# Three more matmuls in twelve attention steps of a fused kernel, one or two fewer in twenty-four

## The chip, the cores and the metric

The kernel runs on one core of a Trainium2 chip. The metric is the device time of one launch in microseconds (us), from the first instruction to the last. Engines are named as in the profile: PE is TensorE (matmuls), PEld its weight loads, DVE is VectorE, ACT is ScalarE, POOL is GpSimd, SP is SyncE, which issues most DMAs.

## The reference

A sparse attention over 8 batches and 8 heads is followed by a two-layer network. In the attention only scores within tau of their row's maximum survive. What is computed, without the set-up:

```python
scores = q @ k.T / sqrt(64)                      # q, k, v: (8, 8, 576, 64)
thresh = max(scores, -1) - tau                   # tau = 0.02
scores = where(scores >= thresh, scores, -1e9)
attn = exp(scores - max(scores, -1)); attn = attn / (sum(attn, -1) + 1e-9)
x = (attn @ v) reordered to (4608, 512)
h = x @ w_in                                     # (512, 2048)
g = h * tanh(softplus(h))
out = g @ w_out                                  # (2048, 512)
```

## The kernel before

**Tiles and steps.** The attention is cut into 288 tiles of 128 rows of q against all 576 keys: 8 batches, 4 pairs of heads in each, 9 tiles a pair. One loop with the number g (line 553) walks over them as a software pipeline. Every engine gets its work in program order: the class InOrder (line 83) chains each engine's instructions, so what stands behind a waiting instruction waits too.

**What PE gets in step g.** First the scores of tile g+1 (`begin`, into an s tile; pss has two of them). Then, in four steps of nine, the product of attention and v for an earlier tile (`product`, nine matmuls into a y tile, lines 406 to 415). Then a number of matmuls of the first product x @ w_in of the previous batch (`advance(stream, n)`, line 645). Last, from step 38 on, the four or five transposes of tile g-2 (line 649; pst has one buffer for them, tp, and one for t5).

**The first product as a stream.** `gemm1` (line 446) is a generator that yields after every matmul. An output tile h has 12 matmuls: four blocks of the inner dimension times three products, since x and w_in are each split in a high and a low part (xh, xl, w1h, w1l). A batch has 32 h tiles, 384 matmuls. After its twelfth matmul an h is copied to hst by ACT (`leave`, line 473). The table MIX_FIRST, MIX or MIX_LAST says how many matmuls step g takes; MIX_FIRST is for the first batch, whose stream runs in steps 42 to 77, and is read at g modulo 36:

```python
advance(stream, DRAIN if g >= NT else MIX_FIRST[(step + 6) % 36] if b == 1 else ...)
```

**What the other engines do in step g.** DVE takes the row maximum of tile g (st), the small operations on it, lo of tile g-3 (the low part of the transposed tile, which needs ACT's hi of the same tile), and p of tile g (the masked exponentials, which frees that tile's s). ACT makes hi and tk of tile g-3, the exponentials e of tile g, the copies x and yo of this step's y (`gather`, line 422), casts of loaded q, k and v, and at the end the copies hst of h tiles that ended in this step. POOL normalises p and makes low parts. Up to step 54 DVE, ACT and POOL also decode w_in into w1h and w1l (the tiles named dec).

**The buffers in question.** The pool psh has two PSUM buffers with the tag "ph". Every h and every y takes one of them, and it is free again once ACT has copied its content out (hst for an h, x and yo for a y).

```python
psh = outer.enter_context(tc.tile_pool(name="psh", bufs=2, space=PSUM))
y = psh.tile([P, 512], F32, name="y", tag="ph")
banks[c, f] = pool.tile([P, 512], F32, name="h", tag=tag)
```

**Behind the loop** w_out is decoded, the gate is applied and the second product (line 848) fills the rest of the span.

Of the kernel before, what the change touches and what calls it, by code (L numbers as in the profile page):

```python
# [64 lines left out]
    8: [(3, 128, 0, 128)],  # L65
}
MIX = (11, 12, 6, 9, 8, 13, 12, 14, 16, 6, 16, 4, 12, 4, 15, 5, 16, 13)
MIX_FIRST = (11, 12, 6, 9, 8, 13, 6, 14, 22, 6, 16, 4, 12, 4, 15, 9, 16, 13, 7, 12, 5, 10, 8, 13, 12, 14, 16, 6, 16, 4, 12, 4, 15, 5, 16, 13)
MIX_LAST = (12, 14, 16, 6, 16, 4, 12, 4, 15, 5, 16, 13, 11, 12, 6, 9, 8, 13, 12, 14, 16, 6, 16, 4, 12, 4, 15, 5, 16, 13, 11, 12, 6, 9, 8, 13)
DRAIN = 18  # L70
LAST = {1: 0, 4: 1, 6: 2, 8: 3}
# [87 lines left out]
def attention_moe(tc, q, k, v, tau, w_in, w_out, out):  # L159
# [3 lines left out]
    with ExitStack() as outer:  # L163
# [12 lines left out]
        with ExitStack() as first:  # L176
# [6 lines left out]
            with ExitStack() as att:  # L183
# [311 lines left out]
                def advance(stream, n):  # L495
                    for _ in range(n):
                        next(stream, None)
# [55 lines left out]
                for g in range(NT + 5):  # L553
# [88 lines left out]
                    if b >= 1:  # L642
                        if step == 0:
                            stream = gemm1(b - 1, batches.pop(b - 1))
                        advance(stream, DRAIN if g >= NT else MIX_FIRST[(step + 6) % 36] if b == 1 else MIX[g % 18] if b < B - 1 else MIX_LAST[step])
                    if g < len(WARM[1]):
# [252 lines left out]
```

## Time and profile before

| what | value |
|---|---|
| median of 3 runs | 1373.96 us |
| lowest and highest run | 1373.25, 1374.07 us |
| profiled execution, its own time | 1371.94 us |
| its span, first to last instruction | 1370.2 us |
| PE, DVE, ACT, POOL busy | 1352.5, 1000.6, 944.0, 774.0 us |
| steps 42 to 77 in the span | 137.5 to 257.3 us |

The profile is one execution on the chip. A row of its timeline gives the start in us from the span's start, the duration, the engine, the line of the kernel (L93 stands for every instruction recorded by the helper InOrder), the operation, output and inputs by the program's names without buffer numbers, the shape, how many equal instructions were merged (x4), and in brackets how long the engine sat idle before and what ended that. A row of the windows gives, for each engine, the busy time and in brackets the number of instructions, then PEclk, the granted TensorE clock as a share of 2.4 GHz, and the share of the DMA engines. The steps are found by DVE's row maxima (TENSOR_REDUCE), one in each step: step 42's starts at 137.48 us, step 78's at 257.32 us.

### The profile page before, as it was taken

How to read it: one execution, taken by the hardware profiler on the slowest of the kernel's cores; microseconds unless marked ns; L12 is line 12 of the kernel's file. 1: busy time of each engine (PE TensorE's matmuls, PEld its weight loads, DVE VectorE, ACT ScalarE, POOL GpSimd, SP SyncE). 2: the span in 40 equal slices, each digit the busy share in tenths (PEclk: the TensorE clock that was granted, in tenths of full speed). 3: DMA queues.
4: the chain of work that ended last, by engine and by line, in shares of the span. 5: the costliest groups of instructions: out<-in, count | busy, mean ns of one | idle time of the engine just before them, and what ended most of it. 6: DMA issues, size and time to landing. Idle time of an engine off the chain costs nothing. (4 is left out here: it accounts for less than half of the span.)

```text
span 1370.2 us, 27693 instructions
## 1 busy us (share of the span) xinstructions
PE 1352.5 (99%) x8839; PEld 1225.8 (89%) x8839; DVE 1000.6 (73%) x2976; ACT 944.0 (69%) x2106; POOL 774.0 (56%) x1115
## 2 busy tenths in 40 slices
PE   9998999999999999999999999999999999999999
PEld 7555899999999999999999999999987888888888
DVE  5999999999999999999999999957874332232210
ACT  5788788888888888888888888856555543443210
POOL 4778888778788787887887878732460000000000
PEclk9999999999999999999999999999999999999999
DMA  4333423333333233332332423128655553543310
GB/s 142 100 96 109 121 79 116 108 96 103 101 99 115 89 121 93 111 105 99 103 111 88 121 93 107 64 86 279 194 164 154 150 151 103 143 132 99 95 52 23
DMA packets 126017, 154.64 MB, mean 113 GB/s; under 512 B 23472, under 2 KB 109488, under 8 KB 125872
## 3 DMA queue, kind: packets, MB, share of 16 engines
q1 hardware_dynamic: 124720, 148.16, 36.2%
q10 hardware_dynamic: 1152, 4.72, 0.9%
q8 instruction: 70, 1.15, 0.3%
q14 instruction: 75, 0.61, 0.1%
HBM read 105.64 MB, written 47.19 MB: 112 GB/s over the span
## 5 line engine op out<-in xcount | busy, mean ns | idle before, releaser
L848 PE MATMUL o<-g,w2h 128*128 128x512 f32 (+1 forms) x1280 | 363.7, 370 | 0.6 <-DVE g L681 0.6
L93 PE MATMUL h<-xh,w1h 128*128 128x288 f32 x1024 | 302.3, 295 | 1.0 <-ACT hst L93 0.6
L93 PE MATMUL h<-xl,w1h 128*128 128x288 f32 x1024 | 302.2, 295 | 0.0
L93 PE MATMUL h<-xh,w1l 128*128 128x288 f32 x1024 | 302.2, 295 | 0.0
L93 POOL TENSOR_SCALAR p<-p,st 128x576 f32<-128x576 f32 x288 | 244.9, 850 | 58.6 <-DVE st L93 37.2
L848 PEld LDWEIGHTS o<-g,w2h 128*128 128x128 f32 x1280 | 231.6, 188 | 43.4 <-DVE g L681 1.1
L93 PE MATMUL s<-k,q 128*128 128x288 f32 (+1 forms) x1280 | 255.0, 324 | 7.9 <-DVE p L93 5.8
L93 DVE SCALAR_TENSOR_TENSOR p<-s,st,e 128x576 f32<-128x576 f32 x288 | 235.0, 816 | 20.6 <-ACT e L93 11.0
L93 ACT ACTIVATE e<-s,st 128x576 f32<-128x576 f32 x288 | 214.4, 744 | 35.5 <-DVE st L93 30.2
L848 PE MATMUL o<-g,w2l 128*128 128x512 f32 (+1 forms) x640 | 236.1, 369 | 0.0
L93 DVE TENSOR_REDUCE st<-s 128x1 f32<-128x576 f32 x288 | 216.6, 752 | 6.7 <-PE s L93 6.6
L93 PEld LDWEIGHTS s<-k,q 128*128 128x128 f32 (+1 forms) x1280 | 182.5, 189 | 37.4 <-DVE p L93 21.8
L93 DVE TENSOR_TENSOR lo<-tp,hi 128x512 fp32r<-128x512 f32 (+1 forms) x280 | 174.7, 632 | 48.0 <-ACT hi L93 41.0
L93 PEld LDWEIGHTS h<-xh,w1h 128*128 128x128 f32 x1024 | 192.6, 188 | 1.9 <-ACT hst L93 1.0
L93 PEld LDWEIGHTS h<-xh,w1l 128*128 128x128 f32 x1024 | 192.5, 188 | 0.0
L93 PEld LDWEIGHTS h<-xl,w1h 128*128 128x128 f32 x1024 | 192.5, 188 | 0.0
L93 PE MATMUL tp<-ident,p 128*128 128x128 f32 x1152 | 174.4, 274 | 3.5 <-DVE lo L93 2.3
L93 ACT CAST hi<-tp 128x512 fp32r<-128x512 f32 (+1 forms) x280 | 149.8, 546 | 36.4 <-PE tp L93 33.5
L681 DVE TENSOR_TENSOR g<-ht,g 128x1024 fp32r<-128x1024 f32 (+1 forms) x60 | 68.6, 1153 | 137.6 <-ACT g L680 137.6
L93 PEld LDWEIGHTS tp<-ident,p 128*128 128x128 f32 x1152 | 139.0, 140 | 13.6 <-issue 5.8
L676 ACT ACTIVATE ht<-ht 128x1024 f32<-128x1024 f32 (+1 forms) x60 | 60.2, 1003 | 115.9 <-DMA ht<-hd 114.5
L848 PEld LDWEIGHTS o<-g,w2l 128*128 128x128 f32 x640 | 120.3, 188 | 21.2
(87 smaller groups left out, 2226.7 us busy)
## 6 DMA issues: line engine op xcount, KB each, us to landing
hd<-hst SPq DMA_DIRECT2D x56, 576.0 KB, 3.3
r<-q SPq DMA_DIRECT2D x120, 160.0 KB, 2.3
r<-k SPq DMA_DIRECT2D x120, 160.0 KB, 2.3
ht<-hd SPq DMA_DIRECT2D x52, 288.0 KB, 3.3
r<-v SPq DMA_DIRECT2D x56, 160.0 KB, 2.3
dec<-w_in SPq DMA_DIRECT2D x32, 256.0 KB, 2.7
out_t<-ost SPq DMA_DIRECT2D x32, 256.0 KB, 2.9
g<-w_out SPq DMA_DIRECT2D x48, 128.0 KB, 2.8
```

The costliest lines, as they stand in the source:

```text
L93: made = method(*args, **kwargs)
L676: nc.scalar.activation(ht, ht, AF.Mish)
L681: engine.tensor_tensor(gl, ht, fv(gh), ALU.subtract)
L848: nc.tensor.matmul(o[:, :m], a, b, start=n == 0, stop=n == 3 * NF - 1)
```

## The change

Only the table MIX_FIRST changes. By the step that reads an entry: steps 42 to 47 and 72 to 77 (the table's entries 6 to 11 and 0 to 5) take three more matmuls each, steps 48 to 71 one or two fewer. The sum of the table goes from 384 to 385, while the stream has 384 matmuls, so step 77 takes 15 where its entry says 16. After step 47 the stream is 18 matmuls ahead of before, after step 59 one ahead, after step 71 seventeen behind. What each matmul computes does not change, and no wait, buffer or DMA is added.

```diff
-MIX_FIRST = (11, 12, 6, 9, 8, 13, 6, 14, 22, 6, 16, 4, 12, 4, 15, 9, 16, 13, 7, 12, 5, 10, 8, 13, 12, 14, 16, 6, 16, 4, 12, 4, 15, 5, 16, 13)
+MIX_FIRST = (14, 15, 9, 12, 11, 16, 9, 17, 25, 9, 19, 7, 10, 3, 13, 8, 14, 12, 5, 11, 4, 9, 6, 12, 10, 13, 14, 5, 14, 3, 10, 3, 13, 4, 14, 12)
```

PE's order at the end of step 43 before: the last matmuls of the step in an h tile (h_1987 is the second of the batch), the transposes (tp, t5), then the scores s of the next step. In brackets stands the engine whose semaphore an instruction waits for (Activation is ACT).

```order
L93 MATMUL h_1987<-xl_1479,w1h_96 128x288
L93 MATMUL tp_1996<-ident_79,p_1830 128x128 [waits DVE_49,PE_49,Pool_49]
L93 MATMUL tp_1996<-ident_79,p_1830 128x128 x3
L93 MATMUL t5_2001<-ident_79,p_1830 128x128
L93 MATMUL s_2003<-k10_1569,q0_1568 128x288 [waits DVE_49]
L93 MATMUL s_2003<-k20_1570,q0_1568 128x288
L93 MATMUL s_2003<-k10_1569,q0_1568 128x288
L93 MATMUL s_2003<-k20_1570,q0_1568 128x288
```

The same place after: the second h tile is complete, and a third one (h_2001) starts before the transposes.

```order
L93 MATMUL h_1987<-xh_1817,w1l_97 128x288
L93 MATMUL h_2001<-xh_752,w1h_96 128x288 [waits Activation_49]
L93 MATMUL h_2001<-xl_753,w1h_96 128x288
L93 MATMUL tp_2004<-ident_79,p_1830 128x128 [waits DVE_49,PE_49,Pool_49]
L93 MATMUL tp_2004<-ident_79,p_1830 128x128 x3
L93 MATMUL t5_2009<-ident_79,p_1830 128x128
L93 MATMUL s_2011<-k10_1569,q0_1568 128x288 [waits DVE_49]
L93 MATMUL s_2011<-k20_1570,q0_1568 128x288
L93 MATMUL s_2011<-k10_1569,q0_1568 128x288
```

What moved: six more h matmuls stand ahead of these transposes (three of step 42, three of step 43), and the first matmul of h_2001, which waits for ACT, stands ahead of the transposes and scores.

PE's order in step 67 before: the last matmul of a y tile (y_3318), four h matmuls, all of one h tile that ends there, then the transposes and the next scores.

```order
L93 MATMUL y_3318<-tk_3156,vs_2286 128x256
L93 MATMUL h_3299<-xh_1480,w1l_97 128x288
L93 MATMUL h_3299<-xh_1819,w1h_96 128x288
L93 MATMUL h_3299<-xl_1820,w1h_96 128x288
L93 MATMUL h_3299<-xh_1819,w1l_97 128x288
L93 MATMUL tp_3354<-ident_79,p_3182 128x128 [waits DVE_49,Pool_49]
L93 MATMUL tp_3354<-ident_79,p_3182 128x128 x3
L93 MATMUL t5_3359<-ident_79,p_3182 128x128
```

The same place after: three h matmuls, of which two end an h tile and the third starts the next.

```order
L93 MATMUL y_3306<-tk_3149,vs_2308 128x256 [waits Activation_49]
L93 MATMUL h_3285<-xl_1820,w1h_96 128x288
L93 MATMUL h_3285<-xh_1819,w1l_97 128x288
L93 MATMUL h_3340<-xh_754,w1h_96 128x288 [waits PE_49,Activation_49]
L93 MATMUL tp_3342<-ident_79,p_3175 128x128 [waits DVE_49,Pool_49]
L93 MATMUL tp_3342<-ident_79,p_3175 128x128 x3
L93 MATMUL t5_3347<-ident_79,p_3175 128x128
L93 MATMUL s_3349<-k11_2539,q1_2538 128x288 [waits DVE_49]
```

What moved: the boundary between two h tiles, which stood in the next step, now stands two matmuls behind y. The same form, an h that ends and one that starts behind a y of the same step, comes up in steps 47, 58, 67, 72 and 76 after, and in no step of 42 to 77 before.

## Rows read from the trace of the kernel before

**Rows 1.** The page, busy time of PE: us, share of the span, instructions.

```profile
PE 1352.5 (99%) x8839; PEld 1225.8 (89%) x8839; DVE 1000.6 (73%) x2976; ACT 944.0 (69%) x2106; POOL 774.0 (56%) x1115
```

**Rows 2.** Windows over steps 42–53, 54–59, 60–71, 72–77 (columns: see above).

```profile
137.50:184.40 46.90, 41.88 (x291) 39.27 (x291) 45.71 (x151) 37.81 (x99) 41.74 (x51) 0.95 0.36 109
184.40:201.90 17.50, 17.50 (x133) 17.11 (x133) 16.69 (x57) 15.00 (x36) 13.79 (x21) 1.00 0.25 73
201.90:239.10 37.20, 37.19 (x286) 36.51 (x285) 33.94 (x115) 31.88 (x79) 32.60 (x50) 1.00 0.39 118
239.10:257.30 18.20, 18.20 (x143) 18.20 (x141) 17.00 (x55) 15.45 (x36) 12.44 (x20) 1.00 0.22 75
```

**Rows 3.** Waits of PE, steps 42 to 59: us in total, times, longest.

```profile
PE s L93 <- DVE p L93: 3.8, 6, 1.2
PE tp L93 <- DVE lo L93: 1.1, 1, 1.1
```

**Rows 4.** Timeline of PE in step 43: start, duration (us), what, idle before.

```profile
143.03 0.30 PE L93 MATMUL h<-xh,w1h 128*128 128x288 f32 x1
...
144.75 0.29 PE L93 MATMUL h<-xl,w1h 128*128 128x288 f32 x1
146.12 0.63 PE L93 MATMUL tp<-ident,p 128*128 128x128 f32 x4 [1.08 <-DVE lo L93]
...
147.25 0.80 PE L93 MATMUL s<-k,q 128*128 128x288 f32 x4 [0.39 <-DVE p L93]
```

**Rows 5.** Timeline of ACT, end of step 43 and start of step 44.

```profile
145.22 0.74 ACT L93 ACTIVATE e<-s,st 128x576 f32<-128x576 f32 x1 [1.87 <-DVE st L93]
...
146.88 0.40 ACT L93 COPY hst<-h 128x288 f32<-128x288 f32 x1
147.17 0.59 ACT L93 CAST hi<-tp 128x512 fp32r<-128x512 f32 x1
```

**Rows 6.** Timeline of DVE, lo in steps 44, 50 and 64.

```profile
148.16 0.67 DVE L93 TENSOR_TENSOR lo<-tp,hi 128x512 fp32r<-128x512 f32 x1
...
171.27 0.69 DVE L93 TENSOR_TENSOR lo<-tp,hi 128x512 fp32r<-128x512 f32 x1 [0.43 <-ACT hi L93]
...
216.32 0.69 DVE L93 TENSOR_TENSOR lo<-tp,hi 128x512 fp32r<-128x512 f32 x1 [0.80 <-ACT hi L93]
```

**Rows 7.** Timeline of PE, transposes and scores behind steps 60 and 64.

```profile
205.58 0.60 PE L93 MATMUL tp<-ident,p 128*128 128x128 f32 x4
205.94 0.78 PE L93 MATMUL s<-k,q 128*128 128x288 f32 x4
...
217.94 0.60 PE L93 MATMUL tp<-ident,p 128*128 128x128 f32 x4
218.55 0.80 PE L93 MATMUL s<-k,q 128*128 128x288 f32 x4
```

**Rows 8.** PE and ACT, y's last matmul and yo, steps 67, 72, 76.

```profile
226.37 0.28 PE L93 MATMUL y<-tk,vs 128*128 128x256 f32 x1
227.08 0.36 ACT L93 COPY yo<-y 64x256 f32<-64x256 f32 x1
...
241.31 0.31 PE L93 MATMUL y<-tk,vs 128*128 128x320 f32 x1
242.09 0.42 ACT L93 COPY yo<-y 64x320 f32<-64x320 f32 x1
...
253.40 0.28 PE L93 MATMUL y<-tk,vs 128*128 128x256 f32 x1
254.20 0.36 ACT L93 COPY yo<-y 64x256 f32<-64x256 f32 x1
```

**Rows 9.** Timeline of PE, step 44, the h behind a wait for hst.

```profile
150.01 0.40 PE L93 MATMUL h<-xh,w1h 128*128 128x288 f32 x1
```

**Rows 10.** Windows around step 43 with the granted clock (PEclk), columns as above.

```profile
131.80:135.20 3.40, 1.42 (x8) 0.98 (x8) 3.31 (x11) 3.34 (x9) 2.19 (x4) 1.00 0.32 95
135.20:142.00 6.80, 5.68 (x24) 5.31 (x25) 6.71 (x23) 5.71 (x16) 6.80 (x10) 0.50 0.41 114
```


## The prediction

> **What bounds the kernel now.** I read the page's busy times first: TensorE (PE) is busy for 99% of the span [rows 1]. Busy PE is not the whole answer, so I next took the windows over steps 42 to 77, the only steps whose numbers change, cut at four places [rows 2]. They show two regimes. In 137.5 to 184.4 us (steps 42 to 53) VectorE (DVE) is busy 45.71 of 46.90 us and PE only 41.88: here w_in is still being decoded, and DVE sets the pace. From 184.4 us on PE has no idle time to speak of (17.50 of 17.50, 37.19 of 37.20, 18.20 of 18.20), yet DVE is close behind (33.94 of 37.20 in steps 60 to 71). Third, the waits of PE by cause: in steps 42 to 59 it sat idle 3.8 us for p of DVE (the score banks) and 1.1 us for lo of DVE (the transpose bank) [rows 3]. That idle time is what extra matmuls could fill.
>
> The pitch of one h matmul is the unit of everything: in step 43 fourteen of them start between 143.03 and 144.75 us, 13 pitches in 1.72 us, so 0.132 us each [rows 4].
>
> **The change in numbers.** By step number modulo 36, steps 42 to 47 get 18 more matmuls (2.38 us of PE), steps 48 to 59 get 17 fewer, steps 60 to 71 get 18 fewer, and steps 72 to 77 get 17 more (step 77 asks for 16, but only 15 of the 384 are left). Nothing is added to any engine, only moved, so the time changes by the waits of PE that appear less those that go. I went through the steps one by one, keeping three clocks (PE, ScalarE = ACT, DVE), with the durations of the trace.
>
> **Early, steps 42 to 59.** Step 42's three extra matmuls move step 43 by 0.40 us. In step 43 the third h tile now starts after 15 matmuls, at 143.03 + 0.40 + 15 x 0.132 = 145.41 us. psh has two buffers, both held by h tiles, and the one it needs was finished 12 matmuls earlier; ACT's copy of it is the last thing ACT does in the step, 146.88 to 147.28 us [rows 5], behind an exponential that waits for DVE and not for PE. So PE waits about 1.9 us there, in place of the wait for lo before the transposes (146.12 us) and the one for p before the scores (147.25 us) [rows 4]. Behind the waiting matmul are queued one more h, the transposes and the scores: the transposes start near 147.7 instead of 146.12 us, the scores near 148.2 instead of 147.25. The six matmuls found no gap. ACT's hi then starts near 148.35 instead of 147.17 us [rows 5], and DVE's lo near 148.95 instead of 148.16 us [rows 6]: DVE, the bound here, is 0.8 us late. Steps 44 to 47 add 12 x 0.132 = 1.58 us, which PE mostly cannot hide in steps 44 to 46 (it hardly waits there now), and in step 47 an h starts five matmuls after a y, of which more below. By step 48 I have PE's scores 1.4 us late and DVE 0.8 to 1.1 us. Steps 48 to 54 stay DVE-bound, and fewer matmuls there mostly lengthen PE's waits. DVE regains something where it now waits for hi (0.43 us at 171.27 [rows 6]), since transposes come earlier. In steps 54 to 59 PE has up to seven matmuls less to do than before, but DVE is busy 16.69 of 17.50 us [rows 2], so at most 0.8 us comes back, and step 58 has a new wait of 0.5. I carry **+0.45 us** into step 60. Bounds: -0.9 if the lead of seven matmuls at step 54 is kept whole and DVE loses nothing; +1.5 if DVE keeps its delay and the new waits come on top.
>
> **Middle, steps 60 to 71.** Eighteen matmuls fewer are 2.38 us of 37.20. Not all can be had: PE already waits for DVE before some scores (218.55 us, 0.61 us behind the transposes, where 0.36 is the pitch without a wait, as 205.94 less 205.58 shows [rows 7]; three more like it follow), and DVE's 33.94 us plus its own wait for hi (0.80 us at 216.32 [rows 6]) leave about 2 us. I take **-1.4 us**, bounds -0.9 and -2.4.
>
> **Late, steps 72 to 77.** PE has no slack here [rows 2], so 17 x 0.132 = **+2.25 us**.
>
> **The new wait: an h behind a y in the same step.** A y takes one of psh's two buffers while the other holds the open h. If that h ends and another starts in the same step, the new one needs the buffer of y or of the h just ended; ACT empties y first (x, then yo), and h after that. Before, no step does this; now steps 47, 58, 67, 72 and 76 do, 5, 5, 2, 4 and 2 matmuls behind y. Price from rows, as the end of yo less the start of y's last matmul, against PE's arrival. Step 67: 227.08 + 0.36 - 226.37 = 1.07 us, PE arrives after 0.12 + 2 x 0.132 = 0.38, wait 0.69 [rows 8]. Step 72: 242.09 + 0.42 - 241.31 = 1.20, arrival 0.15 + 4 x 0.132 = 0.68, wait 0.52 [rows 8]. Step 76: 254.20 + 0.36 - 253.40 = 1.16, arrival 0.38, wait 0.78 [rows 8]. With about 0.1 us each to start again (an estimate: the first h behind the one short wait for hst takes 0.40 us instead of 0.29 [rows 4, 9]) that is 0.8 + 0.6 + 0.9 = **+2.3 us**, all where PE is the bound; those of steps 47 and 58 are already in the early term. Behind each waiting h stand the transposes and scores of the step, so DVE and ACT fall back with PE. Bounds: 1.4 (step 67's falls into a stretch where DVE is late anyway, and step 72's half hidden) and 2.6.
>
> **The clock, a rule against the rows.** The granted clock fell to 0.50 (1.2 GHz) for 135.2 to 142.0 us [rows 10], behind a stretch in which PE made eight matmuls between its waits (busy 1.42 of 3.40 us); through the waits of steps 43 to 54, the longest 1.2 us [rows 3], it stayed at 1.00 (2.4 GHz): the mean of 0.95 in the first window [rows 2] is what those microseconds at 0.50 up to 142.0 make. The change makes one wait of 1.9 us there. The Trainium skill, page "TensorE: Matmul & The Clock Gate", section "A second HAM failure mode: psum-queue depth-cycling", says that a kernel cycling through PSUM buffers can idle PE briefly so often that its clock swings between the two levels; nothing in this trace shows waits on buffers doing that. By the rows I add nothing; as a rival it has a price below.
>
> **Sum.** 0.45 - 1.4 + 2.25 + 2.3 = +3.6 us. Later batches keep their numbers and PE has no slack to give it back. Against the profiled execution (span 1370.2, 1371.94 us in all) that is 1375.5 us; the median of the runs is 1373.96, 2.0 us above the profiled one, and the forecast is set on it: 1373.96 + 3.6 = **1377.6 us**, 0.26% slower.
>
> **Rivals.** (1) The lead pays: the 18 early matmuls fill PE's 4.9 us of idle time [rows 3], the lead of seven at step 54 is kept (-0.9), the middle gives its full 2.4, and ACT empties y early enough that the late waits vanish: -0.9 - 2.4 + 2.25 = -1.0 us, 1372.9 us. For it: the idle time is there, and DVE waits for hi, which earlier transposes shorten. Against it: both buffers of psh are held in the five steps named, and yo's end is a fixed time behind y. It decides from the point at which ACT's copies end before PE arrives. (2) The clock falls once more behind step 43's wait: for 6.8 us, as from 135.2 to 142.0, PE does half its work, 3.4 us less, and as the place is DVE-bound I count half of that, 1.7 us: +5.3 us, 1379.3 us. For it: the wait of 1.9 us is longer than any in steps 43 to 59 now. Against it: none of up to 1.2 us lowered the clock there, and many matmuls follow. (3) Faster by more than 0.2%, that is by over 2.75 us: it would need all 18 early matmuls free (2.4 us), DVE's waits for hi (0.43 us at 171.27 us) gone as well, and no new wait: 1371 us.
>
> **How the numbers follow.** The forecast has 0.61, its own range 1375.4 to 1379.6; rival 1 has 0.22, rival 2 0.14, rival 3 0.03. About 0.2% (2.75 us) is what a measurement of this kernel can tell from no change. Of the forecast's 0.61 a quarter (0.15) lies below 1376.7. Slower: 0.46 + 0.14 = 0.60. Same: 0.15 + 0.22 = 0.37. Faster: 0.03. The range leaves out the lower two thirds of rival 1, rival 3 and the far end of rival 2: 1373.4 to 1379.9.
>
> **What would show it.** In the trace after: a PE wait for ACT's hst of over 1.5 us inside step 43 (right) or none (my reading of psh is wrong); waits of h for ACT's yo of 0.5 to 0.9 us in steps 67, 72 and 76, where there are none now; row maxima (TENSOR_REDUCE) of step 60 about 0.5 us later, of step 78 about 3.6 us later, with no further change up to the end. If step 60 comes earlier than before by half a microsecond or more, the early term is wrong and the lead pays; if the granted clock is 0.50 anywhere behind 142 us, rival 2 holds. If step 78 moves by 3.6 us and the end does not, something later gives time back that I do not see.

## The result and the profile after

The changed kernel takes 1378.49 us (median of six runs, 1377.78 to 1380.14) where the kernel before takes 1374.05 beside it: 1.0036 times as long, with an interval of 1.0026 to 1.0046. A second series gave 1.0040 (1.0028 to 1.0053). The forecast was 1377.6 us, +3.6; the medians say +4.4, the ratios +4.9 and +5.5. The sign, the range and the mechanism of the late steps held. The middle term of the sum was mis-sized, the early one probably too, and what happens in the early steps was told only in part. One of the eleven runs of the early numbers alone (below) took 2665.24 us and counts in no ratio.

The profiled execution of the changed kernel is its slowest run (1380.14 us), and that of the kernel before (1371.94) was a quick one, so the two profiles lie 8.2 us apart. On the page, the line that answers [rows 1]:

```profile
PE 1354.2 (98%) x8839; PEld 1224.8 (89%) x8839; DVE 1001.5 (73%) x2976; ACT 943.6 (68%) x2106; POOL 771.3 (56%) x1115
```

PE is busy 1.7 us more; the rest of the difference is idle time. The windows that answer [rows 2], cut at the row maxima of steps 42, 54, 60, 72 and 78 (stretch and length, busy time of PE, PEld, DVE, ACT and POOL with their instructions, granted clock, DMA share, GB/s):

```profile
137.00:187.80 50.80, 43.39 (x298) 41.28 (x299) 46.99 (x151) 38.29 (x100) 40.85 (x51) 0.93 0.34 100
187.80:205.30 17.50, 16.96 (x126) 16.26 (x126) 16.68 (x55) 15.05 (x36) 13.99 (x22) 1.00 0.25 75
205.30:242.50 37.20, 35.52 (x268) 34.10 (x267) 33.84 (x113) 31.19 (x77) 32.31 (x49) 1.00 0.38 115
242.50:264.20 21.70, 20.59 (x156) 20.12 (x155) 16.95 (x57) 15.93 (x37) 13.66 (x22) 1.00 0.24 75
```

Steps 42 to 53 take 50.80 us instead of 46.90, and steps 72 to 77 take 21.70 instead of 18.20. Steps 60 to 71 have 18 matmuls less and take the same 37.20 us: PE, which had no idle time there, now has 1.68 us of it. The waits of PE, steps 42 to 59 (this answers [rows 3]; us in total, times, longest):

```profile
PE s L93 <- DVE p L93: 4.8, 6, 1.4
PE h L93 <- ACT hst L93: 2.3, 1, 2.3
PE h L93 <- ACT yo L93: 0.7, 2, 0.5
PE tp L93 <- DVE lo L93: 0.5, 1, 0.5
```

The matmuls that were to fill the idle time have not lowered it: the wait for p is longer than before (4.8 against 3.8), and two new kinds stand beside it. The 2.3 us are in step 43, where the timeline of PE (start, duration, what, idle before) reads, answering [rows 4]:

```profile
144.20 0.29 PE L93 MATMUL h<-xh,w1l 128*128 128x288 f32 x1
146.79 0.40 PE L93 MATMUL h<-xh,w1h 128*128 128x288 f32 x1 [2.29 <-ACT hst L93]
...
147.24 1.05 PE L93 MATMUL tp<-ident,p 128*128 128x128 f32 x4
...
148.16 1.31 PE L93 MATMUL s<-k,q 128*128 128x288 f32 x4
```

and ACT at the same place, answering [rows 5]:

```profile
144.71 0.74 ACT L93 ACTIVATE e<-s,st 128x576 f32<-128x576 f32 x1 [2.04 <-DVE st L93]
145.35 0.76 ACT L93 ACTIVATE dec<-dec 128x256 f32<-128x256 f32 x2
146.01 0.44 ACT L93 CAST vs<-r 128x320 fp32r<-128x320 f32 x1
146.36 0.68 ACT L93 COPY hst<-h 128x288 f32<-128x288 f32 x2
```

The third h tile waits for ACT's copy of the first, which stands behind an exponential, two decoding steps and a cast; from the last matmul to the next are 2.59 us, 2.46 more than the pitch of 0.132. Behind it four transposes take 1.05 us and four scores 1.31, where they took 0.63 and 0.80 [rows 4], since the granted clock has fallen to 0.50 (1.2 GHz) behind the wait, at 147.07 us. The windows up to it and in it (columns as above):

```profile
140.25:147.00 6.75, 4.46 (x34) 4.22 (x34) 6.72 (x17) 4.31 (x12) 5.25 (x7) 1.00 0.47 131
147.00:150.50 3.50, 3.50 (x17) 3.48 (x17) 2.26 (x11) 2.18 (x8) 1.22 (x2) 0.51 0.20 51
```

The late waits, PE first and then ACT's yo, in steps 67, 72 and 76 (they answer [rows 8]):

```profile
230.46 0.40 PE L93 MATMUL h<-xh,w1h 128*128 128x288 f32 x1 [0.58 <-ACT yo L93]
245.86 0.40 PE L93 MATMUL h<-xh,w1h 128*128 128x288 f32 x1 [0.43 <-ACT yo L93]
260.23 0.40 PE L93 MATMUL h<-xh,w1h 128*128 128x288 f32 x1 [0.68 <-ACT yo L93]
...
230.04 0.36 ACT L93 COPY yo<-y 64x256 f32<-64x256 f32 x1
245.38 0.42 ACT L93 COPY yo<-y 64x320 f32<-64x320 f32 x1
259.81 0.36 ACT L93 COPY yo<-y 64x256 f32<-64x256 f32 x1
```

Each h starts 0.06 us behind the end of yo (230.46 against 230.04 + 0.36). Counted from the matmul ahead, less the pitch, the waits are 0.75, 0.59 and 0.84 us.

For all later comparisons the starts of DVE's row maxima (TENSOR_REDUCE) cut the program into three stretches, in us; the names are those of the experiments below:

| kernel | steps 42–59 | steps 60–71 | steps 72–78 |
|---|---|---|---|
| before | 64.42 | 37.19 | 21.55 |
| before, again | 65.92 | 37.20 | 21.54 |
| changed | 68.32 | 37.20 | 25.34 |
| changed, again | 68.49 | 37.21 | 25.33 |
| no late waits | 68.16 | 36.61 | 23.67 |
| early numbers | 67.42 | 36.94 | 21.54 |
| late numbers | 65.28 | 37.92 | 25.34 |
| late, no waits | 65.90 | 37.31 | 23.66 |
| three waits in before | 65.37 | 38.60 | 22.55 |
| step 43's wait out | 65.48 | 37.23 | 25.31 |
| step 43's wait in before | 66.71 | 37.19 | 21.56 |
| no waits | 64.74 | 36.49 | 23.65 |
| early, no waits | 66.24 | 36.93 | 21.55 |
| lead of 12 | 66.16 | 36.51 | 21.54 |

The last two columns repeat to 0.02 us between two executions of one kernel. The first does not: it differs by 1.5 us between two executions of the kernel before. Its whole difference lies in a decoding operation of DVE in step 53, which takes 0.87 or 2.41 us (the end of this document); the other steps repeat to 0.1 us. Two more things differ between the profiles. One is the stretch at 1.2 GHz near step 42, which every profile has and which lasts 3.41 or 6.83 us: in the five profiles in which it ended less than 2.8 us behind step 42's row maximum, that step is 0.63 to 0.66 us shorter. The other is a second fall of the clock, of which more below. So the late terms are read from the profiles, the early ones from the timed runs, and from profiles that are alike in these things. Behind step 79 nothing changes up to the end of the loop; the last 1.0 us of the 8.2 comes behind the loop, and in the second profile of the changed kernel that is 0.03.

### The profile page after: what moved, and what is told of

It reads as the page before. It is cut to its first block, busy times and chain, and to the rows that moved or that the text cites. A ratio compares the mean times of both kernels' runs of the same rounds, so it can differ in the third digit from the quotient of the medians.

```text
span 1378.4 us, 27695 instructions
## 1 busy us (share of the span) xinstructions
PE 1354.2 (98%) x8839; PEld 1224.8 (89%) x8839; DVE 1001.5 (73%) x2976; ACT 943.6 (68%) x2106; POOL 771.3 (56%) x1115
## 4 chain that ended last, share of the span: by engine, by line
PE 81%; DVE 6%; ACT 4%; DMA 3%; issue 3%; POOL 2%; SPq 1%; ACTq 0%; DVEq 0%; POOLq 0%
PE h L93 24%; PE o L848 23%; PE s L93 13%; PE y L93 12%; PE tp L93 8%; DMA g<-w_out 1%; DVE st L93 1%; DVE p L93 1%; PE t L93 1%; DVE dec L93 1%; DMA hd<-hst 1%; ACT e L93 1%; POOL w2l L156 1%; DMA out_t<-ost 1%; DVE g L93 1%
## 5 line engine op out<-in xcount | busy, mean ns | idle before, releaser
L93 POOL TENSOR_TENSOR x<-x,yo 64x256 f32<-64x256 f32 (+1 forms) x112 | 89.8, 801 | 90.4 <-ACT yo L93 87.5
```

The costliest lines, as they stand in the source:

```text
L93: made = method(*args, **kwargs)
```

## Experiments

All are other tables of numbers for steps 42 to 77; every kernel computes the same. A diff names the steps and their matmuls. The runs of each series share the runs of before. Ratios are against these, with their intervals; a thousandth is 1.37 us. Lead and lag are the matmuls of the stream by which a kernel is ahead of the kernel before or behind it.

**Early part and late part apart.** The early numbers alone:

```diff
- steps 42 to 59: 6 14 22 6 16 4 12 4 15 9 16 13 7 12 5 10 8 13
+ steps 42 to 59: 9 17 25 9 19 7 10 3 13 8 14 12 5 11 4 9 6 11
```

> Steps 42 to 58 as in the changed kernel, step 59 with 11 matmuls, so that step 60 begins with as many matmuls done as before, and steps 60 to 77 as before. Of the new waits only those of steps 43, 47 and 58 are left. Theory of the prediction, by its early term alone (+0.45, bounds -0.9 to +1.5): 1374.5 us, 0.5 above before. Rival, the clock: the granted clock falls again behind step 43's wait, as in the profiled execution of the changed kernel (147.07 to 150.49 us), where step 60 came 3.9 us later than step 42's shift says: 1376 to 1378 us, and the fall is to be seen in the trace. Rival, the lead pays: 1373 us or less. With the median of the change at +4.4 and its late part forecast at +3.2, I expect about +1.2 of the early part, 1375.3 us.

Measured: 1374.72 against 1373.45, 1.0009 (0.9999 to 1.0018): about +1.2 us (-0.1 to +2.5 by the interval), nearer to the theory's 1374.5 than to the rivals. The clock fell again behind step 43's wait (148.62 to 152.03 us). The late numbers alone:

```diff
- steps 59 to 77: 13 12 14 16 6 16 4 12 4 15 5 16 13 11 12 6 9 8 13
+ steps 59 to 77: 14 10 13 14 5 14 3 10 3 13 4 14 12 14 15 9 12 11 16
```

> Steps 42 to 58 as before, step 59 with 14 matmuls, so that step 60 begins with as many done as in the changed kernel, and steps 60 to 77 as in it: the new waits of steps 67, 72 and 76 stand as there, those of 43, 47 and 58 are gone. Theory of the prediction, by its middle and late terms and these waits (-1.4 + 2.25 + 2.3): +3.2, 1377.2 us; in the profiled execution of the changed kernel steps 60 to 79 made 3.8, so up to 1377.9 us. No second fall of the clock. Rival, all of the loss comes from the early steps and the clock: within 0.5 us of before. Rival, the waits cost but the middle gives its full 2.4: +2.2, 1376.2 us.

Measured: 1377.8, 1.0033 (1.0022 to 1.0045): about +4.5 us, more than the 3.2 to 3.9 expected, and no second fall of the clock. The loss is mainly late; the rival that puts it all into the early steps is out. The parts add up to 5.7 us, beside 4.9 and 5.5 for the whole; a wait that these numbers make in step 59, and that the changed kernel does not have, explains some of it (below).

**The waits for psh.** First the late three taken out of the changed kernel:

```diff
- steps 67, 68: 3 13    steps 71, 72: 12 14    steps 75, 76: 12 11
+ steps 67, 68: 2 14    steps 71, 72: 16 10    steps 75, 76: 14 9
```

> The changed kernel with a few matmuls moved across the border of two neighbouring steps (step 67 gets 2 instead of 3, 68 one more; 71 gets 16 instead of 12, 72 four fewer; 75 gets 14 instead of 12, 76 two fewer), so that in steps 67, 72 and 76 no h starts behind another in a step with a y. Theory of the prediction: the three waits of 0.6 to 0.9 us go, -2.3 us against the changed kernel, 1376.2 us. Rival, the 17 matmuls moved to steps 72 to 77 cost by themselves and the waits are only where PE stands (DVE or ACT late anyway): 1378.2 us or more, the waits come back under another name (p of DVE before the scores). In between means that part of each wait was covered.

Measured: 1376.06, 1.0018 (1.0010 to 1.0027), some 2.5 us less than the changed kernel by the ratios, 1.8 by the medians over before. The windows of steps 60 to 71 and 72 to 77:

```profile
205.50:242.10 36.60, 35.45 (x268) 34.13 (x266) 33.82 (x115) 31.00 (x77) 32.26 (x49) 1.00 0.37 116
242.10:262.10 20.00, 20.00 (x156) 20.00 (x155) 16.99 (x57) 15.97 (x37) 12.48 (x20) 1.00 0.23 72
```

In steps 72 to 77 PE is again without idle time (20.00 of 20.00). From step 60 to 79 the stretches of the table make 62.54 us in the changed kernel and 60.28 here: the three waits cost 2.26 us. Then the same kind of wait put into the kernel before:

```diff
- steps 62 to 64: 16 6 16    steps 66 to 68: 12 4 15    steps 73 to 75: 12 6 9
+ steps 62 to 64: 18 6 14    steps 66 to 68: 14 4 13    steps 73 to 75: 10 6 11
```

> The kernel before with two matmuls moved to the step ahead or behind in three places (62 to 64: 18, 6, 14; 66 to 68: 14, 4, 13; 73 to 75: 10, 6, 11), so that in steps 63, 67 and 74 an h starts 4, 2 and 2 matmuls behind a y, with next to no lead or lag beside it. Theory: each wait costs what it shows in the trace and some 0.1 us to start again, 0.6 + 0.9 + 0.9 = +2.4 us, 1375.9 us. Rival, PE's wait is covered since DVE or ACT is late there anyway, or is regained in the next DVE-bound step: +0.5 us or less.

Measured: 1375.7 against 1373.58, 1.0020 (1.0011 to 1.0029): +2.7 us by the ratio, +2.1 by the medians, and 61.15 - 58.74 = 2.41 us in the table. Two matmuls moved by one step, three times, cost about half of what the whole change does. The waits of PE, steps 60 to 78; the one of step 63 is put down to DVE's st:

```profile
PE h L93 <- ACT yo L93: 1.3, 2, 0.7
PE h L93 <- DVE st L93: 0.4, 1, 0.4
```

Last, the late numbers alone, without their waits:

```diff
- steps 59 to 77: 13 12 14 16 6 16 4 12 4 15 5 16 13 11 12 6 9 8 13
+ steps 59 to 77: 14 10 13 14 5 14 3 10 2 14 4 14 16 10 15 9 14 9 16
```

> Steps 42 to 58 as before, step 59 with 14, steps 60 to 77 with the numbers of the change without the waits of steps 67, 72 and 76 (2, 14; 16, 10; 14, 9). What is left is the middle term and the 17 matmuls of steps 72 to 77. The prediction had -1.4 + 2.25 = +0.85; the profiles of the changed kernel say -0.6 + 2.1 = +1.5, since DVE and not PE sets the pace in steps 60 to 71 once PE has 18 matmuls less: 1375.1 us. Against the same numbers with the three waits: 1.8 to 2.5 us less.

Measured: 1375.36 against 1373.5, 1.0014 (1.0005 to 1.0023): +1.9 us (1.5 expected), where the same numbers with the waits cost +4.5. One wait for psh is left in both runs of late numbers: with 14 matmuls, step 59 opens a second h tile, whose buffer ACT's hst copy empties. PE and ACT in this run:

```profile
202.31 0.30 PE L93 MATMUL h<-xh,w1l 128*128 128x288 f32 x1
202.78 0.40 PE L93 MATMUL h<-xh,w1h 128*128 128x288 f32 x1 [0.17 <-ACT hst L93]
...
202.32 0.72 ACT L93 COPY hst<-h 128x288 f32<-128x288 f32 x2
```

From row maximum to row maximum step 60 takes 3.84 us in both, where the kernel before takes 3.30, and so steps 60 to 71 are no shorter here (37.31) than before. Steps 61 to 71 take 33.47 us instead of 33.89.

**Step 43's wait.** Taken out of the changed kernel:

```diff
- steps 43, 44: 17 25
+ steps 43, 44: 15 27
```

> The changed kernel with two matmuls moved from step 43 to step 44 (15 and 27), so that the third h of step 43 starts in step 44, behind ACT's copy. Theory of the prediction: the wait of 2.5 us for ACT goes, the transposes of step 43 come back to about 146.1 us, DVE isn't late there; of the early term 0.8 us goes, 1377.7 us. Rival, the clock: without the wait the granted clock doesn't fall at 147 us, and 2 to 3.5 us go, 1375 to 1376.5 us. If the clock falls again all the same, the wait is not what brings it.

Measured: 1377.13, 1.0027 (1.0016 to 1.0037), 1.2 us less than the changed kernel by the ratio and 0.8 by the medians over before, nearer to the theory's 0.8 than to the rival's 2 to 3.5. The clock stays up; the window of the whole stretch, and PE's transposes and scores of step 43:

```profile
139.75:152.00 12.25, 11.21 (x84) 10.67 (x84) 12.14 (x38) 8.39 (x23) 9.51 (x13) 1.00 0.42 112
```

```profile
144.82 0.63 PE L93 MATMUL tp<-ident,p 128*128 128x128 f32 x4 [0.58 <-DVE lo L93]
...
146.01 0.81 PE L93 MATMUL s<-k,q 128*128 128x288 f32 x4 [0.45 <-DVE p L93]
```

And put alone into the kernel before:

```diff
- steps 42 to 44: 6 14 22
+ steps 42 to 44: 9 17 16
```

> The kernel before with 9, 17 and 16 matmuls in steps 42 to 44 instead of 6, 14 and 22: the lead of the change in the first two steps and its third h tile in step 43, and everything else as before. Theory: PE waits about 2 us for ACT's copy, the granted clock falls for some 3.4 us near 147 us, and the time is 0.5 to 1.3 us above before (what the early part cost by itself). Rival, the wait alone lowers no clock, the extra matmuls of steps 44 to 47 do: no fall, within 0.4 us of before.

Measured: 1374.22 against 1373.58, 1.0005 (0.9996 to 1.0014): +0.7 us by the ratio, as expected of the theory, though the interval reaches below nothing. Step by step the profile says the same: against the second one of the kernel before, which has the same long decoding operation, step 44 is 1.40 us longer, step 42 is 0.63 shorter, and the rest of steps 42 to 59 is level. The clock falls behind the wait without the rest of the change; PE's waiting matmul and the window behind it:

```profile
145.74 0.46 PE L93 MATMUL h<-xh,w1h 128*128 128x288 f32 x1 [1.76 <-ACT hst L93]
```

```profile
145.75:149.25 3.50, 3.50 (x16) 3.48 (x17) 2.25 (x11) 2.12 (x7) 1.41 (x2) 0.53 0.19 47
```

**All waits for psh taken out** of the changed kernel, so that lead and lag are left alone. There are six of them (steps 43, 47, 58, 67, 72 and 76; the expectation says five):

```diff
- steps 43, 44: 17 25    47, 48: 7 10    58, 59: 6 12    67, 68: 3 13    71, 72: 12 14    75, 76: 12 11
+ steps 43, 44: 15 27    47, 48: 5 12    58, 59: 5 13    67, 68: 2 14    71, 72: 16 10    75, 76: 14 9
```

> The changed kernel with all five waits of an h for psh taken out by moving one to four matmuls over the border of two steps (43, 47, 58, 67, 71/72, 75/76); lead and lag are otherwise those of the change. Theory of the prediction: what is left of the change is early term less its waits, -1.4 and +2.25; with what the runs without the late three waits (+2.6) and without step 43's (0.8 less than the change) show, +1.0 to +1.9 us, 1374.5 to 1375.4 us. Rival, the lead pays once nothing stands in its way: 1373 us or less, that is faster than before.

Measured: 1374.57, 1.0007 (0.9999 to 1.0016): +1.0 us. Of the change's 4.9 some four fifths were waits for psh, with what follows them (the second fall of the clock, where there was one). And the early numbers without their three waits, the rest as before:

```diff
- steps 42 to 59: 6 14 22 6 16 4 12 4 15 9 16 13 7 12 5 10 8 13
+ steps 42 to 59: 9 15 27 9 19 5 12 3 13 8 14 12 5 11 4 9 5 12
```

> Steps 42 to 59 with the numbers of the change, but without the waits of an h for psh in steps 43, 47 and 58 (15, 27; 5, 12; 5, 12), steps 60 to 77 as before. Theory, by the profile of the run without all five waits (steps 42 to 60: +0.3 us, where before took +1.5 in its second profile and 0 in its first): between -1.2 and +0.3, about -0.4, 1373.1 us. The early term of the prediction without its waits is then a small gain. Rival, the lead costs by itself as the early numbers did (+1.3 with the waits, of which +0.6 was step 43's): +0.5 us or more.

Measured: 1373.24 against 1373.5, 0.9991 (0.9982 to 1.0000), -1.2 us by the ratio; -0.3 by the medians. The rival (+0.5 or more) is out by the timed runs. A gain is not shown either: in profiles that are alike in step 53 this lead costs 0.32 us in steps 42 to 59 (66.24 against 65.92 for the second profile of the kernel before; without any wait 64.74 against 64.42 for the first). More matmuls in the DVE-bound steps are next to free by themselves.

**The two kernels again**, for a second profile each.

> The kernel before, unchanged, for a second profiled execution and the spread between equal kernels. The first one (1371.94 us) lies 1.5 to 2 us below the median of the timed runs, and the profiles of the other kernels put step 60 later against it than the medians say. If this is one quick execution: the new profiled one is at 1373 to 1374 us, and its steps 42 to 60 take 1 to 2 us longer, by another stretch at the low clock or by a decoding operation of DVE that is held up. Rival: the first one was ordinary, 1371.5 to 1372.5 us again. Median within 0.5 us of the other runs of before.

Measured: median 1373.89, 1.0001 (0.9992 to 1.0010), the profiled run 1375.09. The first profile was a quick execution. The second took 1.46 us more up to step 42, outside the change, and 1.5 us more in steps 42 to 59, all of it at one decoding operation of DVE. Six profiles of other kernels show this operation as long (2.4 us), so that for them the second profile is the one to compare with.

> The changed kernel, unchanged, a second profiled execution and its median beside the same runs of before. Theory: step 43's wait of 2 us or more for ACT's copy and the fall of the granted clock behind it (about 3.4 us) are there again, as in the three profiles that had this wait, and the three late waits of 0.6 to 0.85 us as well; median +3.9 to +4.9 against before. Rival: the second fall of the clock is a thing of single executions, and isn't there in this one.

Measured: median 1379.65 over five runs, 1.0040, +6.2 us by the medians, above what I expected. All waits are there again, but the clock did not fall behind step 43's wait of 1.76 us (put down to p here, but the h starts 0.05 us behind ACT's copy). It fell later, at 183.43 us, at the end of a wait of 3.28 us for p that the scores at 183.62 us end; PE's two waiting instructions and the windows up to the fall and in it:

```profile
146.04 0.40 PE L93 MATMUL h<-xh,w1h 128*128 128x288 f32 x1 [1.76 <-DVE p L93]
...
183.62 0.61 PE L93 MATMUL s<-k,q 128*128 128x288 f32 x1 [3.28 <-DVE p L93]
```

```profile
139.25:183.25 44.00, 36.04 (x268) 34.09 (x266) 42.50 (x127) 33.73 (x89) 37.42 (x46) 1.00 0.35 107
183.25:187.00 3.75, 3.38 (x14) 3.38 (x15) 3.75 (x14) 1.39 (x3) 2.13 (x3) 0.54 0.09 33
```

**A version that beats both.** A lead of one whole h tile, so that the order of h and y in psh stays that of the kernel before:

```diff
- steps 42 to 47: 6 14 22 6 16 4     steps 61, 62, 66, 68, 70: 14 16 12 15 16
+ steps 42 to 47: 9 15 27 9 16 4     steps 61, 62, 66, 68, 70: 12 14 8 13 14
```

> A version that keeps the order of h and y in psh as before: steps 42 to 47 do 12 matmuls more (9, 15, 27, 9, 16, 4), a whole h tile, steps 48 to 59 and 72 to 77 have the numbers of before, and steps 61, 62, 66, 68 and 70 do the 12 fewer (12, 14, 8, 13, 14). No h starts behind another in a step with a y. Theory: PE's idle time in the DVE-bound steps takes the 12 matmuls (1.6 us) for 0 to 0.3 us, and steps 60 to 71 give back 0.4 to 0.7 us up to DVE's pace: -0.1 to -0.7 us, 1373.2 us. Rival, the 12 matmuls cost in steps 42 to 47 what they give back later: 0 to +0.6 us.

Measured: 1372.2 against 1373.5, 0.9987 (0.9976 to 0.9998): -1.8 us by the ratio, -1.3 by the medians, more than expected, with an interval that ends just below 1. The profile shows -0.45 of it, as expected: +0.24 in steps 42 to 59 against the second profile of the kernel before, -0.69 in steps 60 to 71. The window of steps 60 to 71, 36.50 us where the kernel before takes 37.20:

```profile
203.60:240.10 36.50, 35.79 (x274) 34.84 (x273) 33.90 (x115) 31.51 (x79) 32.46 (x50) 1.00 0.38 121
```

PE is busy 1.40 us less than in [rows 2], and half of that becomes time; the other half becomes idle PE.

## Why the prediction was right, and where it was not

**The new wait, +2.3 us: right.** Forecast were 0.69, 0.52 and 0.78 us and 0.1 each to start again; found were 0.75, 0.59 and 0.84 with the restart, and 2.26 us in the stretch from step 60 to 79. The kernel without these waits and the kernel before with three of them (2.41 us) confirm the price from both sides. The working by the end of yo against PE's arrival is what carried the forecast.

**Late matmuls, +2.25 us: right.** Without the waits, steps 72 to 78 take 23.67 and 23.65 us instead of 21.55: +2.1. Between these row maxima stand 16 of the 17 matmuls, 2.11 us at 0.132.

**Middle, -1.4 us: mis-sized, and outside its bounds (-0.9, -2.4).** Without the late waits steps 60 to 71 take 36.61 and 36.49 instead of 37.19: -0.6 to -0.7, and steps 61 to 71 alone 0.4 to 0.5 less, with the late numbers alone too. The step that failed is the slack: I added DVE's busy time and one wait for hi and took the rest of 37.20 us for PE's to give. But at several scores PE then stands still, as behind step 66 of the changed kernel, where they start 1.27 us behind the transposes (0.36 is the pitch without a wait [rows 7]):

```profile
226.49 0.60 PE L93 MATMUL tp<-ident,p 128*128 128x128 f32 x4
227.76 0.66 PE L93 MATMUL s<-k,q 128*128 128x288 f32 x3 [0.67 <-DVE p L93]
```

Four more of 0.3 to 0.4 us, counted in the same way, make 2.3 us in all, where the kernel before has 0.7. So of the 2.38 us that the 18 matmuls give, 1.6 go into standing still at the scores and 0.75 into step 67's wait, and the stretch stays at 37.20 us. DVE is the bound step by step, before its share of the stretch says so.

**Early, +0.45 us: probably too small.** Step 43 went as read: a wait of 2.46 us for ACT's copy (forecast 1.9) in place of the waits for lo and p. The early numbers alone cost about +1.2 us, inside the bounds of -0.9 to +1.5; their interval (-0.1 to +2.5) holds 0.45 too. Without the waits of steps 43, 47 and 58 they give -1.2 by the ratio, -0.3 by the medians and +0.32 by profiles alike in step 53. So the waits there, with what follows them, are worth some 1 to 2.4 us, and I had counted 0.8 of delay to DVE and 0.5. One thing I left out stands in the next point. A count was off as well: the lead is nine matmuls when step 54 begins (18 less 9) and seven only when it ends, so that the lower bound should have been -1.2; nothing else hangs on it.

**The clock: rival 2 happened, at half its length.** I added nothing for it, since waits of up to 1.2 us had not lowered it. In four of five profiles with step 43's wait the granted clock fell behind it, and in none of the nine without it did it fall there; the run with this one wait shows that the rest of the change is not needed for it. The second profile of the changed kernel shows that the wait does not always bring it. Nor does its length alone decide: a wait of 1.76 us was followed by the fall in one profile and not in another, and in the seven profiles with the long decoding operation of step 53 PE waited 1.62 to 1.75 us for p behind it, and the clock stayed at 1.00. The fall lasts 3.4 us, half of what the rival took. Its price: from step 44 to step 49 the first profile of the changed kernel, with the fall, took 1.65 us more than the second, without it; the rival had 1.7. At step 60 both profiles are level again, since the second met another delay of DVE's and a fall of the clock behind it. So the time of 1378.49 us lies between the forecast (1377.6) and rival 2 (1379.3), that of the second series (1379.65) above both, and how much of it the clock makes in the median run isn't settled.

**Rival 1, the lead pays: wrong here.** It needed ACT's copies to end before PE arrives, and in all six places they do not. Where no h waits for psh, the lead does fill idle time: in the kernel with a lead of 12, these matmuls are 1.58 us of PE and make steps 42 to 59 only 0.24 us longer.

**The sum.** With the measured terms it is 1.2 - 0.65 + 2.1 + 2.26 = +4.9 us, what the first ratio says. Middle and early were off in the same direction, so that the forecast came out low and no error made up for another.

**What would show it.** Step 60 was to come 0.5 us later and step 78 3.6 us. Against step 42, step 60 came 2.4 to 4.1 us later in the profiles, according to which executions are set beside each other, and step 78 5.9 to 7.5 us; the stretch from step 60 to 79 grew by 3.8 us in both (the prediction's middle, late and wait terms without the early one: 3.15). The sign of rival 2, a clock of 0.50 behind 142 us, was met in both profiles (at 147 and at 183 us). That later batches give nothing back is borne out.

## What to carry to other kernels

When work of one pipe is moved between steps, first count at which place in each step a buffer is opened and who empties the one before it: here six openings in the wrong place cost some four fifths of the loss, and a lead of one whole tile has none of them. A share of busy time close to one (33.94 of 37.20 us) can be a bound in single steps already, so count the waits of the single steps: here 0.6 to 0.7 of the 3.3 us that the sum of busy times leaves came back. Take a second profile of both kernels before terms of a microsecond are read from one, and compare step by step.

## What the hardware showed that I had not expected

**A decoding operation of DVE can last until several operations of POOL are done.** The operation that made the kernel before 1.5 us slower in its second profile, DVE first and POOL's operations of that time below it:

```profile
183.92 2.41 DVE L93 TENSOR_SCALAR dec<-dec 128x256 uint32<-128x256 uint32 x1
...
183.84 0.83 POOL L93 TENSOR_SCALAR p<-p,st 128x576 f32<-128x576 f32 x1
184.63 0.86 POOL L93 TENSOR_TENSOR vs<-r,vs 128x320 fp32r<-128x320 f32 x1
185.45 0.72 POOL L93 TENSOR_TENSOR w1l<-dec,w1h 128x256 fp32r<-128x256 f32 x1
```

It ends at 186.33 us, 0.16 behind POOL's third operation. In the first profile of the same kernel the same operation took 0.87 us and ended 0.15 behind one operation of POOL:

```profile
182.49 0.87 DVE L93 TENSOR_SCALAR dec<-dec 128x256 uint32<-128x256 uint32 x1
...
182.39 0.82 POOL L93 TENSOR_SCALAR p<-p,st 128x576 f32<-128x576 f32 x1
```

The longest stood in the second profile of the changed kernel, ahead of PE's wait of 3.28 us:

```profile
179.09 2.93 DVE L93 TENSOR_SCALAR dec<-dec 128x256 f32<-128x256 f32 x1
...
178.73 0.76 POOL L93 TENSOR_TENSOR dec<-dec 128x256 uint32<-128x256 uint32 x1
179.46 0.84 POOL L93 TENSOR_SCALAR p<-p,st 128x576 f32<-128x576 f32 x1
180.25 0.81 POOL L93 TENSOR_TENSOR xl<-x,xh 128x288 fp32r<-128x288 f32 x1
181.00 0.87 POOL L93 TENSOR_TENSOR k<-r,k 128x320 fp32r<-128x320 f32 x1
```

It ends 0.15 us behind the last of them. Over an execution such operations take 0.32 us in the median (the kernel before, again; ns, least, median and most of 64):

```profile
L93 DVE TENSOR_SCALAR dec<-dec x64: 273/319/2407, 25.0 to 183.9; 128x256 f32<-128x256 f32 x32, 128x256 uint32<-128x256 uint32 x32
```

In the fourteen profiles 143 of these operations took more than 0.7 us, and every one ended 0.15 to 0.16 us behind an operation of POOL. Each operation of POOL that one sits through adds some 0.8 us, in steps where DVE sets the pace, and how many there are differs between executions of one kernel. That POOL is what holds DVE up is read from these ends; no run took POOL's operations away. How much of the spread of the timed runs comes from it was not tried. The Trainium skill, page "SBUF — State Buffer", section "Who interferes with whom", says that VectorE in a two-port mode and GpSimd take a shared pair of ports in turn, and that the later one is blocked until the first is done. The ends 0.15 us behind an operation of POOL agree, though no row tells in which mode DVE decodes. That a waiting DVE also lost to two and three operations which POOL began later is not in the rule; the rows decide.

**One wait can lower the clock.** Step 43's waits of 1.76 to 2.3 us, in steps in which PE otherwise works, were followed by 3.4 us at 1.2 GHz in four profiles of five; the late waits of 0.4 to 0.7 us never were, and the waits of 1.62 to 1.75 us for p behind step 53's decoding neither. What decides is open, and so is why the clock stayed up in the fifth profile. One of these waits, in the second profile of the kernel before, with the window behind it:

```profile
187.12 0.80 PE L93 MATMUL s<-k,q 128*128 128x288 f32 x4 [1.64 <-DVE p L93]
```

```profile
187.12:195.00 7.88, 7.88 (x57) 7.62 (x58) 7.54 (x27) 6.06 (x14) 6.08 (x9) 1.00 0.28 93
```

The Trainium skill, page "TensorE: Matmul & The Clock Gate", section "A second HAM failure mode: psum-queue depth-cycling", ties such swings to frequent short idling between banks; here one long wait for a bank was followed by it, and the few short ones by nothing.
